# Tied scaling passes in a layer norm, later transposes, and twelve plain chunks instead of fourteen in an attention and GLU kernel

## The chip, the cores and the metric

The kernel runs on one core of a Trainium2 chip. The metric is device time of one execution in microseconds (us); the time before is the median of three runs. One execution was also taken with the hardware profiler, and all rows below are of that execution. Five engines work side by side: TensorE (PE, matrix products and transposes), VectorE (DVE), ScalarE (ACT), GpSimd (POOL) and SyncE (SP, which here only issues DMAs). Each engine runs its own instructions strictly in the order of its list, and waits at the head of the list when an operand is not there yet.

## The reference

Everything is fp32, with S = 2048 tokens of D = 576, 32 heads of 18, a window of 8 positions at distance 2, and F = 4608.

```python
def _A_ref(x, wqkv, wo):
    q, k, v = split_heads(x @ wqkv)
    idx = pos[:, None] - (jnp.arange(8) * 2)[None, :]
    logits = jnp.einsum("bhsd,bhswd->bhsw", q, k[idx]) * Dh ** -0.5   # masked where idx < 0
    o = jnp.einsum("bhsw,bhswd->bhsd", softmax(logits), v[idx])
    return o.reshape(B, S, D) @ wo
def _B_ref(x, w_gate, w_up, w_down):
    return (sigmoid(x @ w_gate) * (x @ w_up)) @ w_down
h = x + _A_ref(_layernorm(x), A_wqkv, A_wo)
return h + _B_ref(_layernorm(h), B_w_gate, B_w_up, B_w_down)
```

(`split_heads` and `k[idx]` stand for the reshapes and gathers of the reference.)

## The kernel before

Tokens are cut into four blocks of 512 (0 to 3). Every fp32 operand is split into a high and a low part (`split`: a copy on ACT, L104, and a subtraction on DVE, L105), and a product is made of three matrix products (high·high, low·high, high·low). A "token" product is the projection of 128 tokens (14 matmuls with 432 or 288 columns, lines 157 to 160); the four transposes that bring 128 normalised tokens into contraction order are line 146 and the small fifth one is line 150.

The program has these stages.

1. The front: the norm of a block (`ln1`) gives tiles `th` and `tl`; `qkv` projects it for one group of eight heads (four token products, copied out by ACT on line 397, stored to DRAM). For blocks 0 and 1 the norm's statistics are on DVE (`ln_j`). For blocks 2 and 3 they are on ACT and POOL: `ln_stats` makes a sum and a sum of squares (lines 133 and 134), POOL a power (135 to 137), and `ln_scale` two ACT passes (141 the scaling, 142 a copy of 64 columns). `norm_under` puts the norm of the next block between the token products of a `qkv`: block 2 under `qkv(1, 0)`, block 3 under `qkv(1, 1)`. Attention (`attention`, lines 189 to 226, nearly all DVE) of blocks 0 and 1 is stepped in between by `step(ag, n)`; `front` finishes block 0 (projection, norm).
2. The MLP. F is cut into 36 chunks of 128. A **std** chunk treats one block (`single`: 28 matmuls of 128x512 on lines 634 and 641), a **pair** chunk treats two blocks with seven products instead of eight (`pair`: 50 such matmuls). The down product of a chunk and a block is 24 matmuls of 128x288 on line 748, in the queue of `units`, on average one chunk later. The order is the list `items`: std of block 0 for the chunks below `NSTD`, pairs of blocks 0 and 1 for the chunks from there on, std of block 1 for the chunks below `NSTD`, and last all 36 pairs of blocks 2 and 3, whose down product has a form with seven products as well.
3. Under this a background (`bg`) is stepped. In the first std chunks, `under_first` ends the attention of block 1, projects it (`proj_scr`: loads `oj` from the attention's store in DRAM, transposes it, four token products for each half, residual, norm, transposes) and makes the pair's operands (`operands`: `s1` to `s4`). During the pairs, `under_rest` does the attention of blocks 2 and 3 (yielding `ATT`), and in the second std chunks it projects blocks 2 and 3 and makes the operands for the last pairs. `twice` calls `bg_step` eight times in a std chunk (six places, two of them twice).

The weights of a chunk are one load `wg` of 928 KB on SP (L590), issued as soon as its buffer is free, and split in `weights` (tiles `w`, `d`, 640, 256 and 384 columns a piece). The loads of the background (`oj`, `wow`, `hj`, L595) go through `paced`, which ties each behind the last load issued on the same queue. A tied instruction (`issue_after`) keeps its place behind another in the scheduler. The order of all else is set by the scheduler from the order of the code, priorities (`high_priority`), and when tiles come free.

Of the kernel before, what the change touches and what calls it, by code (L numbers as in the profile page):

```python
# [17 lines left out]
AF = mybir.ActivationFunctionType  # L18
# [3 lines left out]
P = 128  # L22
S = 2048
D = 576
# [6 lines left out]
NS = 4  # L31
# [19 lines left out]
END = object()  # L51
ATT = object()
HI = 400
HC = 700
NSTD = 14
NPL = 4
LAG = 3

# [2 lines left out]
def kernel(ctx, tc, x, wqkv, wo, wmlp, out):  # L61
# [41 lines left out]
    def split(hi, lo, src):  # L103
        act.activation(hi, src, AF.Copy)  # L104
        splits.append(dve.tensor_tensor(lo, src, f32(hi), ALU.subtract))  # L105

    def split_rest(t, src):
        act.activation(t, src, AF.Copy)
        dve.tensor_tensor(t[64:128], src[64:128], f32(t[64:128]), ALU.subtract)
# [20 lines left out]
    def ln_stats(xj, junk):  # L130
        mv = sm.tile([P, 2], F32, bufs=4, name="mv")
        rstd = sm.tile([P, 1], F32, bufs=4, name="rstd")
        act.activation(junk[:, :D], xj, AF.Copy, scale=-1.0 / D, accum_out=mv[:, 0:1])
        act.activation(junk[:, :D], xj, AF.Square, bias=mv[:, 0:1], accum_out=mv[:, 1:2])
        pool.tensor_scalar(rstd, mv[:, 1:2], 1.0 / D, EPS, ALU.mult, ALU.add)
        pool.tensor_tensor(rstd, rstd, mhalf, ALU.pow)
        pool.tensor_tensor(mv[:, 0:1], mv[:, 0:1], rstd, ALU.mult)
        return mv[:, 0:1], rstd

    def ln_scale(xj, nr, xn):  # L140
        act.activation(xn[:, :D], xj, AF.Identity, bias=nr[0], scale=nr[1])
        act.activation(xn[:, D:DX], xn[:, DM:D], AF.Copy)

    def tr_main(ps, xn):
        for c in range(4):
            pe.transpose(ps[:, c * P:(c + 1) * P], xn[:, c * P:(c + 1) * P], ident)
        return ps.rearrange("p (c n) -> p c n", c=4)

    def tr_rest(ps, xn):
        pe.transpose(ps[:, :P], xn[:, DM:DX], ident)  # L150
        return ps[:, :P]
# [193 lines left out]
    def ln1(b, xb):  # L345
        th = th3_tile(F32R) if b == 3 else th_tile()
        tl = tl_tile()
        yield th, tl
        xn = tok_tile()
        pri = 2 * HI if b == 0 else 0  # L350
        nr = []
        for j in range(NS):
            js = slice(j * P, (j + 1) * P)
            while b > 1 and len(nr) < min(j + 2, NS):
                nr.append(ln_stats(xb[:, len(nr)], xn[:, len(nr)]))
            with tc.high_priority(pri):
                if b > 1:
                    ln_scale(xb[:, j], nr[j], xn[:, j])
                else:
                    ln_j(xb[:, j], xn[:, j])  # L360
            pv = tr_main(mm_tile(), xn[:, j])
            pr = tr_rest(acc_tile(), xn[:, j])
            with tc.high_priority(pri):
                split(th[:, 0:4, js], tl[:, :, js], pv)
                split_rest(th[:, 4, js], pr)
            yield

    def raw_w(g):
# [21 lines left out]
    def qkv(b, g, T, w):  # L390
        e, hf = BLOCKS[b]
        ev = ev_tile([P, 3, NS, CG])
        for j in range(NS):
            ps = acc_tile()
            passes.append(tok_major(ps, NQ, *T, slice(j * P, (j + 1) * P), w[:, 0], w[:, 1]))
            with tc.high_priority(HI):
                act.activation(ev[:, :, j], ps[:, :NQ].rearrange("p (t c) -> p t c", t=3), AF.Copy)  # L397
# [36 lines left out]
    ag = att_all()  # L434
    T = []

    def norm_under(b, xb, call, n):
        gl = ln1(b, xb)
        T.append(next(gl))
        for _ in call:  # L440
            step(ag, n)
            next(gl, END)
            step(ag, n)
        drain(gl)

# [10 lines left out]
    w.append(qkv_w(1))  # L456
    xb = load_x(1)
    pads(0)
    norm_under(1, xb, qkv(0, 1, T[0], w[1]), 0)
    pads(1)  # L460
    xb = load_x(2)
    norm_under(2, xb, qkv(1, 0, T[1], w[0]), 1)
    xb = load_x(3)
    norm_under(3, xb, qkv(1, 1, T[1], w[1]), 1)
    wr = raw_w(2)
    heads(((2, 0), (3, 0)), w, 2)
    w.append(qkv_w(2, wr))
    wr = raw_w(3)
    pads(2)
# [373 lines left out]
    def proj_scr(pj, b, raw, wos, ins=None, after=None):  # L843
        e, hf = BLOCKS[b]
        th, tl = th_tile(), tl_tile()

        def tile_j(t, j):
            js = slice(j * P, (j + 1) * P)

            def put(pv, cs):  # L850
                if cs.start == 0:
                    if b < 2:
                        pool.dma_start(hacc[b][:, j], t[1])
                    else:
                        rows = slice(0, 7, 6) if b == 2 else slice(2, 5, 2)
                        pool.dma_start(hsev[:, j // 2, rows, j % 2],
                                       t[1].rearrange("p (i n) -> p i n", i=2))
                act.activation(raw[:, cs, js], pv, AF.Copy)

            yield from proj_j(bg_bank, t, wos, th[:, :, js], tl[:, :, js], lambda: t[0], put, (1, 0))  # L860

        todo = []
        if ins is None:
            ins = []
            for j in range(NS):
                ins.append([load_j(pj, b, j, 0), None])
                for _ in range(3 if b == 1 else 4):
                    yield
            ww = pj.tile([P, 2, 5, DH2], F32R, name="wow")
            paced(f32(ww), wscr[0])  # L870
            wos[0] = ww[:, 0], ww[:, 1]
            yield
            yield
            todo = list(range(NS))
        live = [tile_j(t, j) for j, t in enumerate(ins)]
        n = 0
        for _ in range(5):
            for gn in live:
                if todo and n % 2:
                    j = todo.pop(0)  # L880
                    ins[j][1] = load_j(pj, b, j, 1)
                n += 1
                next(gn)
                yield
        nxt = []
        for j, gn in enumerate(live):
            yield from gn
            if after is not None:
                nxt.append([load_j(pj, after, j, i) for i in range(2)])
        if b == 1:  # L890
            act.dma_start(xscr[b], raw[:, 0:2])
        return nxt
# [20 lines left out]
    def under_first():  # L913
        wos = [None, None]
        for _ in ag:
            if c >= 3 and wos[1] is None:
                wos[1] = wos_early()
            yield ATT
        at_stk.close()
        a1 = xt.tile([P, 5, TB], F32, tag="th", bufs=3, name="ar")  # L920
        with sb_pool("pj", "right") as pj:
            while c < 6:
                yield
            yield from proj_scr(pj, 1, a1, wos)
        with sb_pool("pp", "right") as pp:
            yield from operands(pp, 0, X, ("s2", "s3", "s1", "a11", "s4"), None, a1)
# [196 lines left out]

    def twice(i):
        bg_step(i)
        if i in (1, 4):
            bg_step(i)

    for c, (kind, p, f) in enumerate(items):
# [119 lines left out]
```

## Time and profile before

| | |
|---|---|
| device time, median of 3 | 1589.78 us (1589.67 to 1592.79) |
| profiled execution, device time | 1589.84 us |
| its span in the trace | 1588.0 us |
| granted TensorE clock, mean | 0.997 |
| PE busy | 1553.6 us (98%) |
| DVE busy | 1262.2 us (79%) |
| ACT busy | 872.7 us (55%) |

The span runs from the first to the last instruction of the trace; the device time is 1.84 us more. In the trace, "L157" is a line of the kernel, "acc<-qw,th" its output and inputs, and the bracket at the end of a row is the idle time before it and what released it. A chain shows in order of time which piece waited for which; the waits are grouped by waiting engine and releaser.

### The profile page before, as it was taken

The numbers are of one execution on the slowest core, as the hardware profiler recorded it, in microseconds if no ns is written. First come the engines' busy times: TensorE is split into PE (matmuls) and PEld (weight loads), VectorE is DVE, ScalarE is ACT, GpSimd is POOL, SyncE is SP. The second block draws the span as 40 slices with busy tenths as digits, with TensorE's granted clock in tenths as the row PEclk, the third lists the DMA queues.
The fourth block names the chain that finished last, engine by engine and source line by source line (L and its number), as shares of the span: only waits on it lengthen the run. The fifth ranks groups of instructions, "written<-read, shape, count | busy, mean of one in ns | idle before, by whom it ended". The sixth has DMA issues, their size and how long they took to land.

```text
span 1588.0 us, 22369 instructions
## 1 busy us (share of the span) xinstructions
PE 1553.6 (98%) x8532; PEld 1381.1 (87%) x8532; DVE 1262.2 (79%) x1891; ACT 872.7 (55%) x1568; POOL 193.7 (12%) x245
## 2 busy tenths in 40 slices
PE   7899999999999999999999999999999999999998
PEld 6899987888888888888889988888888888888887
DVE  6989999769999999999446678876677776677755
ACT  5632334425555565666443345776777676677761
POOL 1200000011000001000101100112111211112110
PEclk9999999999999999999999999999999999999999
DMA  7546554526467665665864234899889989989983
GB/s 273 204 155 216 215 184 165 205 81 256 109 161 198 163 160 155 167 176 148 217 195 153 90 112 121 181 181 180 172 175 188 176 171 182 176 168 184 183 173 120
DMA packets 76892, 273.50 MB, mean 172 GB/s; under 512 B 8336, under 2 KB 14224, under 8 KB 75888
## 3 DMA queue, kind: packets, MB, share of 16 engines
q0 software_dynamic: 27648, 104.94, 36.0%
q1 hardware_dynamic: 41504, 147.01, 27.2%
q10 hardware_dynamic: 7632, 20.12, 3.3%
q8 instruction: 67, 1.10, 0.3%
q14 instruction: 41, 0.34, 0.1%
HBM read 145.88 MB, written 128.52 MB: 173 GB/s over the span
## 4 chain that ended last, share of the span: by engine, by line
PE 86%; DVE 8%; DMA 3%; ACT 1%; issue 1%; POOL 1%; SPq 0%; ACTq 0%; DVEq 0%; POOLq 0%
PE b L634 41%; PE dp L748 14%; PE dp L810 11%; PE b L641 8%; PE acc L157 7%; PE b L157 1%; PE bgp L157 1%; DMA wg<-in_wmlp_dram 1%; DVE lg L193 1%; DVE pr L215 1%; DVE w L105 1%; PE acc L160 1%; PE acc L159 1%; DVE tl L105 1%; DVE pr L189 1%
## 5 line engine op out<-in xcount | busy, mean ns | idle before, releaser
L634 PE MATMUL b<-tl,w 128*128 128x512 f32 x1704 | 432.4, 393 | 0.0
L634 PEld LDWEIGHTS b<-tl,w 128*128 128x128 f32 x1704 | 308.8, 188 | 55.5 <-DVE s L654 0.3
L634 PE MATMUL b<-th,w 128*128 128x512 f32 x1356 | 349.4, 393 | 0.9 <-DVE s L723 0.8
L634 PEld LDWEIGHTS b<-th,w 128*128 128x128 f32 x1356 | 247.0, 188 | 46.7 <-DVE s L723 1.3
L104 ACT ACTIVATE w<-wg 128x384 fp32r<-128x384 f32 (+2 forms) x194 | 115.7, 598 | 119.8 <-PE b L641 59.4
L816 ACT ACTIVATE ev<-dp 128x576 f32<-128x576 f32 x224 | 144.9, 647 | 62.9 <-PE dp L810 58.6
L641 PE MATMUL b<-th,w 128*128 128x512 f32 x568 | 175.7, 390 | 0.0
L819 POOL DMA_DIRECT2D h<-ev x128 | 110.1, 860 | 458.5 <-ACT ev L816 442.6
L157 PE MATMUL acc<-qw,th 128*128 128x432 f32 x512 | 156.1, 366 | 1.6 <-DVE qw L105 1.2
L105 DVE TENSOR_TENSOR w<-wg,w 128x384 fp32r<-128x384 f32 (+2 forms) x194 | 125.2, 650 | 38.1 <-ACT w L104 38.0
L105 DVE TENSOR_TENSOR w<-tw,w 128x512 fp32r<-128x512 f32 x116 | 79.6, 687 | 81.3 <-ACT w L104 80.3
L641 PEld LDWEIGHTS b<-th,w 128*128 128x128 f32 x568 | 106.7, 188 | 23.4
L748 PE MATMUL dp<-d,h1h 128*128 128x288 f32 x640 | 120.0, 297 | 0.0
L748 PE MATMUL dp<-d,h0h 128*128 128x288 f32 x608 | 112.5, 295 | 0.8 <-DVE tail L758 0.8
L157 PEld LDWEIGHTS acc<-qw,th 128*128 128x128 f32 x512 | 98.1, 192 | 6.7 <-DVE qw L105 1.5
L748 PEld LDWEIGHTS dp<-d,h1h 128*128 128x128 f32 x640 | 99.6, 190 | 2.9
L756 ACT ACTIVATE stage<-dp 128x576 f32<-128x576 f32 x96 | 61.8, 647 | 66.0 <-PE dp L748 65.6
L748 PEld LDWEIGHTS dp<-d,h0h 128*128 128x128 f32 x608 | 93.6, 189 | 3.9 <-DVE tail L758 1.0
L104 ACT ACTIVATE w<-tw 128x512 fp32r<-128x512 f32 x116 | 72.8, 628 | 41.2 <-PE b L634 40.8
L157 PE MATMUL acc<-qw,tl 128*128 128x432 f32 x256 | 93.4, 365 | 0.0
L397 ACT ACTIVATE ev<-acc 128x432 f32<-128x432 f32 x64 | 33.9, 531 | 100.4 <-PE acc L160 93.9
L189 DVE TENSOR_TENSOR pr<-kw,q 128x2304 f32<-128x2304 f32 x32 | 81.7, 2552 | 3.2 <-DMA kw<-k 3.0
(292 smaller groups left out, 2938.6 us busy)
## 6 DMA issues: line engine op xcount, KB each, us to landing
h<-ev POOLq DMA_DIRECT2D x96, 576.0 KB, 7.3
wg<-in_wmlp_dram SPq DMA_DIRECT2D x49, 928.0 KB, 5.1
h<-stage POOLq DMA_DIRECT2D x24, 1152.0 KB, 10.2
wg<-in_wmlp_dram SPq DMA_DIRECT2D x36, 640.0 KB, 4.3
kw<-k SPq DMA_DIRECT2D x16, 792.0 KB, 4.7
vw<-v SPq DMA_DIRECT2D x16, 792.0 KB, 4.7
wd<-in_wmlp_dram SPq DMA_DIRECT2D x18, 576.0 KB, 7.4
h<-ev POOLq DMA_DIRECT2D x32, 288.0 KB, 6.7
```

The source lines that it names most:

```text
L104: act.activation(hi, src, AF.Copy)
L105: splits.append(dve.tensor_tensor(lo, src, f32(hi), ALU.subtract))
L157: pe.matmul(ps[:, :n], a[:, c, js], m[:, c], start=k == 0, stop=False)
L189: dve.tensor_tensor(pr, both(kw, u), q[:, us].unsqueeze(2).broadcast_to([P, 2, W, CG]), ALU.mult)
L397: act.activation(ev[:, :, j], ps[:, :NQ].rearrange("p (t c) -> p t c", t=3), AF.Copy)
L634: pe.matmul(ps, wt[:, a, k0 + c], xx[:, m + c], start=first and k == 0, stop=k == 5, skip_group_check=True)
L641: pe.matmul(ps, wt[:, a, k0], xx[:, 4], start=False, stop=a == 1, skip_group_check=True)
L748: pe.matmul(ps[:, i, :DH2], a[:, js], d[:, m, i * DH2:(i + 1) * DH2], start=k == 0, stop=k == n)
L756: act.activation(hv, ps, AF.Copy)
L810: pe.matmul(ps[:, i, :DH2], a[x][:, js], m[y], start=k in (0, 1, 3) and q == 0, stop=q == 2, skip_group_check=True)
L816: act.activation(hs[:, k % 2], ps[:, :, :DH2], AF.Copy)
L819: pool.dma_start(hsev[:, u, k0:k + 1], hs[:, :k + 1 - k0], accum_op=ALU.add, max_dma_last_dim=8 * D)
```

## The change

It has four parts.

- `NSTD` goes from 14 to 12. The list `items` has 84 entries instead of 86: chunks 12 and 13 of blocks 0 and 1, which were two std chunks of block 0 and, later, two of block 1, become two pair chunks.
- `twice` calls `bg_step` ten times in a std chunk instead of eight when the last step was not one of the attention. The first `proj_scr` starts from chunk 5 and not 6; its `oj` loads are 4 (block 1) or 7 (block 2) steps apart and not 3 or 4.
- In the norms of blocks 2 and 3 the scaling pass (L141) is tied behind the Square pass (L134) of the next tile.
- The transposes of those norms lag two tiles behind the scaling. The last two tiles of block 2 are transposed within `norm_under` of block 3 (ahead of its first transposes), the last two of block 3 under `qkv(2, 0)`.

```diff
-NSTD = 14
+NSTD = 12
...
     def ln1(b, xb):
...
+        lag = 2 if b > 1 else 0
         nr = []
-        for j in range(NS):
-            js = slice(j * P, (j + 1) * P)
-            while b > 1 and len(nr) < min(j + 2, NS):
-                nr.append(ln_stats(xb[:, len(nr)], xn[:, len(nr)]))
...
+        for k in range(NS + lag):
+            if k < NS and b > 1:
+                while len(nr) < min(k + 2, NS):
+                    nr.append(ln_stats(xb[:, len(nr)], xn[:, len(nr)]))
+                with tc.issue_after(getattr(nr[-1][2], "ins", nr[-1][2])):
+                    ln_scale(xb[:, k], nr[k], xn[:, k])
+            elif k < NS:
+                with tc.high_priority(pri):
+                    ln_j(xb[:, k], xn[:, k])
+            if k >= lag:
+                j = k - lag
...
-    def norm_under(b, xb, call, n):
+    def norm_under(b, xb, call, n, before=()):
         gl = ln1(b, xb)
         T.append(next(gl))
         for _ in call:
             step(ag, n)
+            drain(before)
             next(gl, END)
             step(ag, n)
-        drain(gl)
+        return gl
...
-    norm_under(2, xb, qkv(1, 0, T[1], w[0]), 1)
+    gl = norm_under(2, xb, qkv(1, 0, T[1], w[0]), 1)
     xb = load_x(3)
-    norm_under(3, xb, qkv(1, 1, T[1], w[1]), 1)
+    gl = norm_under(3, xb, qkv(1, 1, T[1], w[1]), 1, gl)
     wr = raw_w(2)
-    heads(((2, 0), (3, 0)), w, 2)
+    for _ in qkv(2, 0, T[2], w[0]):
+        next(gl, END)
+        step(ag, 2)
+    heads(((3, 0),), w, 2)
...
-                for _ in range(3 if b == 1 else 4):
+                for _ in range(4 if b == 1 else 7):
                     yield
...
-            while c < 6:
+            while c < 5:
                 yield
...
     def twice(i):
         bg_step(i)
-        if i in (1, 4):
+        if i in (1, 4) or phase is not ATT and i in (2, 5):
             bg_step(i)
```

The change moves instructions; three places are shown. The first is PE in the front, right behind the first token product of `qkv(1, 0)`, where `mm<-ident,tok` is a transpose of block 2 and `acc<-qw,th` a token product of block 1. Before:

```order
L157 MATMUL acc<-qw,th 128x432
L159 MATMUL acc<-qw,th 128x432
L160 MATMUL acc<-qw,th 128x432
L146 MATMUL mm<-ident,tok 128x128 x4
L150 MATMUL acc<-ident,tok 128x128
L157 MATMUL acc<-qw,th 128x432
```

With the change, at the same place:

```order
L157 MATMUL acc<-qw,th 128x432
L159 MATMUL acc<-qw,th 128x432
L160 MATMUL acc<-qw,th 128x432
L157 MATMUL acc<-qw,th 128x432
L157 MATMUL acc<-qw,tl 128x432
L157 MATMUL acc<-qw,th 128x432 x2
```

The transposes of block 2's first tile have left this place and stand two token products later; the others of blocks 2 and 3 lag likewise, and each pair of token products that they leave is run back to back.

The second is PE in the first std chunks, at the first transpose of the projection of block 1 (`b<-ident,oj`); `b<-tl,w` and `b<-th,w` are gate or up matmuls, and `dp` the down product. Before:

```order
L634 MATMUL b_2844<-tl,w_2744 128x512 x6
L634 MATMUL b_2844<-th,w_2743 128x512 x6
L641 MATMUL b_2844<-th,w_2743 128x512 x2
L146 MATMUL b_2898<-ident,oj 128x128 x4
L748 MATMUL dp<-d,h0h 128x288 x2
L748 MATMUL dp<-d,h0l 128x288 x2
```

With the change:

```order
L642 MATMUL b_2864<-tl,w_2752 128x512 x4
L146 MATMUL b_2832<-ident,oj 128x128 x4
L642 MATMUL b_2864<-tl,w_2752 128x512 x2
L146 MATMUL bgp<-ident,oj 128x128 x4
L642 MATMUL b_2864<-th,w_2751 128x512 x3
L146 MATMUL b_2871<-ident,oj 128x128 x4
L642 MATMUL b_2864<-th,w_2751 128x512 x2
L146 MATMUL bgp<-ident,oj 128x128 x4
L642 MATMUL b_2864<-th,w_2751 128x512
L649 MATMUL b_2864<-th,w_2751 128x512 x2
```

It is the same group of 14 gate and up matmuls (`b_2844`, now `b_2864`): the first transpose stood behind all 14, and now stands behind four, so ten of them come after it; the other three follow within the group, where they were spread over the next chunk.

The third is ACT in the second std chunks, at the copies of the transposes of block 2 (`th<-b`, `th<-bgp`) among the splits of the weights (`w<-wg`). Before:

```order
L678 ACTIVATE s<-b_7600 128x512
L104 ACTIVATE th<-b_7620 128x4x128
L104 ACTIVATE w_7709<-wg 128x640
L756 ACTIVATE stage<-dp 128x576
L104 ACTIVATE th<-bgp 128x4x128
L104 ACTIVATE w_7589<-wg 128x256
L104 ACTIVATE th<-b_7656 128x4x128
L104 ACTIVATE w_7588<-wg 128x384
L104 ACTIVATE th<-bgp 128x4x128
```

With the change:

```order
L104 ACTIVATE d<-wg 128x576
L104 ACTIVATE th<-b_7836 128x4x128
L686 ACTIVATE s<-b_7828 128x512
L104 ACTIVATE th<-bgp 128x4x128
L104 ACTIVATE th<-b_7862 128x4x128
L104 ACTIVATE w_7991<-wg 128x640
L104 ACTIVATE th<-bgp 128x4x128
L108 ACTIVATE th<-b_7906 128x128
L104 ACTIVATE w_7817<-wg 128x256
```

A 640-column split of newly loaded weights stood behind the first of the four copies, and a further one now stands behind the third; the first three copies have none between them. On SP the loads of the projection of block 2 there change from two `oj`, `wg`, two `oj`, `wg`, `wow`, three `hj`, `wg`, `hj` to two `oj`, `wg`, `oj`, `wg`, `oj`, `wow`, `wg`, four `hj`. In the first std chunks, where a `wg` stood behind the first of four `hj`, it now stands behind all four.

More of the change, by code (lines that the diff above doesn't have):

```diff
@@ L133, in ln_stats @@
         act.activation(junk[:, :D], xj, AF.Copy, scale=-1.0 / D, accum_out=mv[:, 0:1])
-        act.activation(junk[:, :D], xj, AF.Square, bias=mv[:, 0:1], accum_out=mv[:, 1:2])
+        sq = act.activation(junk[:, :D], xj, AF.Square, bias=mv[:, 0:1], accum_out=mv[:, 1:2])
         pool.tensor_scalar(rstd, mv[:, 1:2], 1.0 / D, EPS, ALU.mult, ALU.add)
@@ L137, in ln_stats @@
         pool.tensor_tensor(mv[:, 0:1], mv[:, 0:1], rstd, ALU.mult)
-        return mv[:, 0:1], rstd
+        return mv[:, 0:1], rstd, sq
     def ln_scale(xj, nr, xn):
@@ L350, in ln1 @@
         pri = 2 * HI if b == 0 else 0
+        lag = 2 if b > 1 else 0
         nr = []
-        for j in range(NS):
-            js = slice(j * P, (j + 1) * P)
-            while b > 1 and len(nr) < min(j + 2, NS):
-                nr.append(ln_stats(xb[:, len(nr)], xn[:, len(nr)]))
[L356 to L365, printed above, removed]
+        for k in range(NS + lag):
[9 more added lines that the diff above has]
+                j = k - lag
+                js = slice(j * P, (j + 1) * P)
+                pv = tr_main(mm_tile(), xn[:, j])
+                pr = tr_rest(acc_tile(), xn[:, j])
+                with tc.high_priority(pri):
+                    split(th[:, 0:4, js], tl[:, :, js], pv)
+                    split_rest(th[:, 4, js], pr)
             yield
@@ L458 @@
     pads(0)
-    norm_under(1, xb, qkv(0, 1, T[0], w[1]), 0)
+    drain(norm_under(1, xb, qkv(0, 1, T[0], w[1]), 0))
     pads(1)
     xb = load_x(2)
-    norm_under(2, xb, qkv(1, 0, T[1], w[0]), 1)
+    gl = norm_under(2, xb, qkv(1, 0, T[1], w[0]), 1)
     xb = load_x(3)
-    norm_under(3, xb, qkv(1, 1, T[1], w[1]), 1)
+    gl = norm_under(3, xb, qkv(1, 1, T[1], w[1]), 1, gl)
     wr = raw_w(2)
-    heads(((2, 0), (3, 0)), w, 2)
+    for _ in qkv(2, 0, T[2], w[0]):
+        next(gl, END)
+        step(ag, 2)
+    heads(((3, 0),), w, 2)
     w.append(qkv_w(2, wr))
```

## The prediction

> **What bounds the kernel now.** I read the busy times first, then PE's waits, then the stretches in which these waits fall, and last the chain around each.
>
> ```profile
> PE 1553.6 (98%) x8532; PEld 1381.1 (87%) x8532; DVE 1262.2 (79%) x1891; ACT 872.7 (55%) x1568; POOL 193.7 (12%) x245
> ```
>
> PE is the bound over the whole, so a change can only do two things: take matmuls away, or close the few holes in PE. The waits name the holes. (The columns are the waiting instruction, its releaser, total us, times, longest; the 9.1 us at the start, which nothing here touches, is left out.)
>
> ```profile
> PE bgp L146 <- DVE tl L105: 3.4, 1, 3.4
> PE mm L146 <- ACT tok L141: 2.6, 1, 2.6
> PE mm L157 <- DVE tl L105: 1.8, 1, 1.8
> PE acc L150 <- ACT tok L142: 1.8, 2, 1.0
> PE acc L157 <- DVE qw L105: 1.2, 1, 1.2
> PE bgp L150 <- DVE th L109: 1.1, 1, 1.1
> ```
>
> The rows of L141 and L142 are the norms of blocks 2 and 3: transposes that wait for the scaling on ACT, 2.6 + 1.8 = 4.4 us. The two `bgp` rows are the projections under the std chunks. Stretch by stretch (PE, PEld, DVE, ACT and POOL busy, granted clock, DMA share, GB/s):
>
> ```profile
> 40.00:300.00 260.00, 247.85 (x1309) 227.33 (x1309) 246.44 (x281) 100.57 (x217) 18.25 (x27) 0.99 0.52 183
> ...
> 40.00:60.00 20.00, 18.23 (x105) 16.88 (x105) 19.39 (x21) 14.07 (x38) 7.51 (x12) 1.00 0.65 223
> 60.00:80.00 20.00, 17.43 (x87) 16.15 (x87) 19.46 (x20) 10.05 (x25) 3.78 (x6) 0.91 0.54 183
> 300.00:320.00 20.00, 19.54 (x115) 16.75 (x113) 10.74 (x18) 8.72 (x18) 0.00 (x0) 1.00 0.77 295
> 320.00:340.00 20.00, 18.85 (x127) 17.91 (x128) 11.29 (x25) 3.69 (x7) 1.50 (x2) 1.00 0.17 63
> 800.00:820.00 20.00, 16.35 (x95) 13.92 (x94) 8.23 (x14) 9.22 (x18) 1.18 (x1) 0.99 0.90 281
> 820.00:840.00 20.00, 20.00 (x121) 18.68 (x122) 10.40 (x20) 6.33 (x14) 0.00 (x0) 0.92 0.24 88
> ```
>
> In the front (40 to 300) DVE is as full as PE, 246.4 against 247.9 of 260 us, and in the norms' two stretches fuller. Two stretches also run under a lowered clock. Cut to their edges, they and the stretches ahead of them are:
>
> ```profile
> 65.00:68.74 3.74, 1.17 (x8) 0.66 (x6) 3.65 (x4) 1.38 (x3) 2.63 (x3) 1.00 0.23 46
> 68.74:72.15 3.41, 3.41 (x12) 3.23 (x13) 3.25 (x6) 1.91 (x6) 0.00 (x0) 0.50 0.99 357
> 819.68:823.09 3.41, 3.15 (x13) 3.14 (x14) 2.70 (x6) 2.07 (x4) 0.00 (x0) 0.50 0.49 190
> ```
>
> So a hole in PE, 2.57 us idle out of 3.74, is followed by 3.41 us at half clock, which loses another 1.7 us. The 3.4 us hole at 819 has the same tail.
>
> **Part by part. Chunks.** The chain gives the price of a chunk (start, duration, count):
>
> ```profile
> 441.68 3.18 PE dp L748 x24
> 459.42 3.18 PE dp L748 x24
> ...
> 771.21 2.74 PE b L634 x12
> ...
> 790.35 2.74 PE b L634 x12
> ```
>
> The two `b` rows stand two std chunks apart, 19.14 us, so one is 9.57; the two `dp` rows stand one pair apart, 17.74. Two std chunks become one pair, twice: 2 x (17.74 - 19.14) = **-2.8 us**. PE was full in these stretches, so all of it counts.
>
> **Norms.** With the transposes two tiles behind the scaling, a token product of 2.7 us or two stand between; 4.4 us of waits and the 1.7 us of clock at 68.74 should go, 6.1 us on PE. But DVE decides when the attention of block 1 ends, and PE's gain reaches it at one place only:
>
> ```profile
> 88.55 0.66 DVE L205 TENSOR_REDUCE rs<-lg 128x32 f32<-128x256 f32 x1 [3.76 <-ACT lg L203]
> ...
> 87.68 0.53 ACT L397 ACTIVATE ev<-acc 128x432 f32<-128x432 f32 x1 [2.22 <-PE acc L160]
> 88.11 0.41 ACT L203 ACTIVATE lg<-lg 128x256 f32<-128x256 f32 x1
> ```
>
> DVE is idle 3.76 us because the exponential (L203) stands in ACT's list behind the copy of a token product (L397) that waits for PE. With PE 6.1 us ahead, the copy is early and the gap is what the exponential takes with its two hand-overs, some 0.45 us (0.41 and the start): DVE gains **-3.3 us**. The rest of PE's 6.1 comes back as wait: PE reaches the `qw` wait (1.2 us) earlier and waits about 1.2 + 6.1 - 3.3 = 4.0 us there.
>
> **The first std chunks.** From the attention's end a chain runs through two DMAs to the first transpose of the projection:
>
> ```profile
> 296.12 0.68 DVE kw L226
> ...
> 297.72 5.39 DMA o<-kw
> 303.25 2.80 DMA oj<-o
> 306.09 0.66 PE b L146 x4
> ```
>
> It moves 3.3 us up with DVE, to 302.8. In PE's new order this transpose has ten gate and up matmuls behind it that stood ahead of it, 10 x 2.74/12 = **+2.3 us** that PE still has to do when `oj` lands: it waits there for about that long, a wait that before has not. The 1.1 us wait of `bgp` L150 after it, and a shorter one behind that, came from
>
> ```profile
> 310.30 7.67 DMA wg<-in_wmlp_dram
> ...
> 321.13 0.31 DVE th L109
> ```
>
> weights landing late, with the copies of the transposes behind their split. All four `hj` are now ahead of the next `wg` and the split stands later in the lists, so I count **-1.5 us** (the idle PE time of the two stretches, 0.46 + 1.15, is the same). Against it, the products of the four tiles come one after the other with nothing between: each needs its copy, subtraction and residual first. The bounds are 0.5 (one hand-over of 0.3 to 0.5, as L109) and 3 us (a wait like that at 319 twice); I take **+1.5**, nearer to the wait that I saw.
>
> **The second std chunks.** Here is the largest hole:
>
> ```profile
> 805.93 10.52 DMA wg<-in_wmlp_dram
> ...
> 810.03 0.59 ACT L104 ACTIVATE th<-b 128x512 fp32r<-128x512 f32 x1
> 816.47 0.74 ACT L104 ACTIVATE w<-wg 128x640 fp32r<-128x640 f32 x1 [5.85 <-DMA wg<-in_wmlp_dram]
> ...
> 817.64 0.59 ACT L104 ACTIVATE th<-bgp 128x512 fp32r<-128x512 f32 x1
> ```
>
> ACT waits 5.85 us for weights that took 10.52 us, and the copy of a transpose is queued behind it; PE idles 3.65 us in 800 to 820 and loses 0.08 x 20 = 1.6 to the clock, 5.3 in all. In the new order the copies of two tiles have no such split ahead of them, the transposes come about 20 gate and up matmuls later, and the `oj` loads are spread. One split still stands ahead of the copy of the fourth. **-5.3 us**, and for what is left of it 0 to 5 (the whole again); I take **+1.5**: by the order its load is issued at about the first of the four transposes and the split's turn comes about 6 us later, an estimate from the matmuls between, while such loads land as this row of the page (count, size, median us) and the 10.52 above say:
>
> ```profile
> wg<-in_wmlp_dram SPq DMA_DIRECT2D x49, 928.0 KB, 5.1
> ```
>
> Mostly in time, then, and sometimes 4 us late.
>
> **Pair starts and other loads.** Two chunks fewer lie ahead of each start of pairs, so the operands (`s2`, first needed) have less time. Before, the third `bgp` transpose was at 357.18 and `s2` done at 370.9:
>
> ```profile
> 357.18 0.27 PE L150 MATMUL bgp<-ident,oj 128*128 128x128 f32 x1
> 369.65 1.22 DVE L105 TENSOR_TENSOR tl<-rs,tl 128x1024 fp32r<-128x1024 f32 x1
> ```
>
> 13.7 us. In the new order 84 gate and up matmuls (19.2 us) and 48 of the down product (6.4) lie between, 25.6 us: hidden. Without that cover it would cost up to those 13.7. For the second pairs it is 64 and 48, 21 us, against the same chain: hidden. The two more adds of 1152 KB into DRAM and the two fewer `wg` I count with small waits elsewhere at **+0.5** (-0.5 to 3, a wait like those above either way).
>
> **Sum.** -2.8 - 3.3 + 2.3 - 1.5 + 1.5 - 5.3 + 1.5 + 0.5 = -7.1 us. The span of 1588.0 becomes 1580.9, and the profiled time 1589.84 (1.84 beside its span, and 0.06 over the median of the runs) becomes **1582.8**. Its own bounds are 1.0 + 1.5 + 1.0 below and 1.5 + 3.5 + 2.5 above: 1579.3 to 1590.3.
>
> **A rule beside the rows.** The clock fell to 0.50 behind a longest gap of 2.58 us. The Trainium skill, "TensorE: Matmul & The Clock Gate", Part 1, says that the gate looks at a free-running window of about 3.4 us, and in its section on oscillation that gaps above about 3.4 us are to be avoided. The window's length agrees with the 3.41 us of the rows; the limit on a gap does not, since 2.58 was enough. By the limit the 4.0 us wait at `qw` would halve the clock and the 2.3 us wait at `oj` would not; by the rows either may.
>
> **Rivals.**
> (1) *The front gives nothing.* The gap of 3.76 us stays because another ACT entry or a load takes the exponential's place. For it: DVE also waits for loads in the front. Against: the gap's only releaser is that one row. +3.3: 1586.1.
> (2) *The whole of PE's gain arrives.* DVE has slack that its busy time hides, so that -6.1 takes the place of -3.3 + 2.3, and the dense products cost nothing, so that the +1.5 falls: 6.6 less, 1576.2. Against: DVE's 19.4 and 19.5 of 20 us in the norms.
> (3) *The clock follows the moved holes.* The wait at `oj` is over 2 us; one half-clock window behind it costs 1.7: 1584.5. (One at `qw` is eaten by the 1.8 us wait of `mm L157` behind it.)
> (4) *Slower: weights late again and again.* Twelve chunks carry the steps of fourteen, so loads and copies stand closer. Among the loads of 795 to 820 is
>
> ```profile
> wow<-wo SPq DMA_DIRECT2D x1, 1440.0 KB, 14.2
> ```
>
> and with the change a `wg` is right behind the `wow` on SP. If ACT's splits wait for `wg` ahead of transposes, each such place costs what 815 did, 5.3. One in the second std chunks instead of my 1.5, one more behind `wow`, and one in the first std chunks: 3 x 5.3 - 1.5 = +14.4, 1597.2. Two such places still give 1591.9, no change; from the third on it decides. Against: half of all `wg` land within 5.1 us.
>
> That the edit does nothing is out: the matmuls of four std chunks are gone from PE's order, those of two pairs are new, and the transposes have moved.
>
> **How the numbers follow.** 0.2% (3.2 us, about what a measurement can tell) is 1586.6 to 1593.0. Chances: forecast 0.50, (1) 0.17, (2) 0.13, (3) 0.10, (4) 0.10. Faster: nearly all of the forecast and of (3), all of (2), half of (1): 0.76. Slower: (4), 0.10. The rest, 0.14, is the same. The range goes to 1576 to hold (2), and above to 1591.5, the forecast's bound with (1) and a part of (4).
>
> **What would show it.** Right: no PE wait for `tok` L141 or L142 and no half clock near 68; a DVE gap under 1 us at L205 near 85; a PE wait of about 2 us for `oj`; no `bgp` wait over 1.5 us near 800; chunks at 9.57 and 17.74. Wrong: a PE wait over 3 us at a pair's start or in the std chunks with ACT standing at `w<-wg`, or DVE ending block 1's attention no earlier than 296.

## The result: 1586.72 us, 0.19% faster, less than half of what was forecast

| | before | changed |
|---|---|---|
| device time, median of 22 runs each | 1590.18 us | 1586.72 us |
| lowest to highest | 1585.66 to 1593.85 | 1583.3 to 1591.97 |
| ratio | | 0.9981, 95% interval 0.9973 to 0.9989 |
| profiled execution | 1589.84 us | 1591.97 us |

The gain is 3.0 us by the ratio (1.7 to 4.3) where 7.1 were forecast. The direction was right; the size was not. The changed kernel's first profiled execution is the longest of its 22, so a second one was taken (`again` below, 1586.86 us). Where the two traces differ, both numbers are given.

PE's waits in the changed kernel, largest first, without the start (in the first of the two executions):

```profile
PE acc L157 <- DVE qw L105: 2.8, 1, 2.8
PE b L146 <- DMA oj<-o: 2.8, 1, 2.8
PE mm L157 <- DVE tl L105: 2.7, 1, 2.7
...
PE b L146 <- DVE tl L105: 1.8, 1, 1.8
...
PE b L642 <- ACT s L712: 1.6, 1, 1.6
...
PE b L642 <- ACT s L722: 1.1, 2, 0.7
```

The waits for `tok` from L141 and L142 are gone, and so is the 3.4 us wait of `bgp`. In their place stand a longer wait for `qw`, the new one for `oj`, 1.8 us left in the second std chunks, and two that the prediction did not have: L712 and L722, which are copies of PSUM banks inside the **pairs**. The stretches that answer to those of before:

```profile
40.00:60.00 20.00, 20.00 (x114) 19.11 (x113) 19.48 (x19) 14.06 (x37) 3.05 (x9) 1.00 0.64 223
60.00:80.00 20.00, 19.43 (x107) 17.93 (x106) 19.43 (x21) 10.62 (x27) 5.11 (x6) 1.00 0.53 186
300.00:320.00 20.00, 17.25 (x93) 14.65 (x92) 11.02 (x20) 6.62 (x14) 0.00 (x0) 0.83 0.68 250
440.00:460.00 20.00, 18.40 (x101) 15.95 (x101) 16.69 (x17) 8.36 (x15) 1.58 (x2) 1.00 0.63 192
460.00:480.00 20.00, 19.32 (x104) 16.48 (x103) 19.86 (x29) 14.01 (x23) 1.20 (x1) 1.00 0.57 109
840.00:860.00 20.00, 18.03 (x118) 16.23 (x117) 12.73 (x23) 7.88 (x17) 0.00 (x0) 1.00 0.46 169
```

The norms' stretches, 40 to 80, are nearly full (20.00 and 19.43 of 20) and at full clock. PE is short of work in 300 to 320, with a clock of 0.83, and in 440 to 480, where before it was at 20.00 of 20. The 18.03 in 840 to 860 is what is left of the hole in the second std chunks.

To see where the sum failed, the trace is cut at the first gate matmul of a chunk (us; the last column ends with PE's last matmul). Two std chunks are 19.1 us less and two pairs 35.5 more, so "before, counted for 12" is what the second row would show if nothing but matmuls had changed.

| kernel | up to first std | first std | pairs of 0, 1 | second std | last pairs |
|---|---|---|---|---|---|
| before (14) | 231.6 | 155.0 | 384.5 | 185.6 | 626.8 |
| before, counted for 12 | 231.6 | 135.9 | 420.0 | 166.5 | 626.8 |
| changed | 231.1 | 138.0 | 423.9 | 163.3 | 629.4 |
| changed, `again` | 227.4 | 137.4 | 424.5 | 163.5 | 627.8 |

The second std chunks gained 3.0 to 3.2 us, the first lost 1.5 to 2.1, and the **pairs lost 3.9 to 4.5**. That is the larger part of the miss. It lies in three pairs: the sixth, the seventh and the last but one take 19.65, 18.95 and 18.75 us in the first execution and 21.57 (with half clock in it), 17.78 and 18.53 in `again`, where an undisturbed pair takes 17.75.

One boundary has moved with the work. The second std chunks hold 54 matmuls of the down product less (336 for 390), of which two chunks fewer account for 48; the other six stand in the last pairs (1584 for 1578). At 3.18 us for 24 that is 0.8 us, so like for like the second std chunks gained 2.2 to 2.4 us, and 0.8 of the last pairs' loss is work that came to them.

### The profile page after: what moved, and what is told of

It is laid out like the page before. It is cut to its first block, busy times and chain, and to the rows that moved or that the text cites. A ratio compares the mean times of both kernels' runs of the same rounds, so it can differ in the third digit from the quotient of the medians.

```text
span 1590.2 us, 22348 instructions
## 1 busy us (share of the span) xinstructions
PE 1554.2 (98%) x8520; PEld 1381.3 (87%) x8520; DVE 1258.0 (79%) x1889; ACT 877.4 (55%) x1576; POOL 193.7 (12%) x247
## 4 chain that ended last, share of the span: by engine, by line
PE 65%; DMA 4%; issue 3%; DVE 3%; ACT 1%; POOL 0%; SPq 0%; POOLq 0%; DVEq 0%; ACTq 0%
PE b L642 34%; PE dp L818 11%; PE dp L756 11%; PE b L649 6%; DMA wg<-in_wmlp_dram 2%; PE b L157 1%; PE bgp L157 1%; DVE w L105 1%; DMA h<-ev 1%; DMA tail<-h 0%; DMA o<-kw 0%; DVE s L662 0%; ACT w L104 0%; PE b L146 0%; DVE lg L193 0%
## 5 line engine op out<-in xcount | busy, mean ns | idle before, releaser
L104 ACT ACTIVATE w<-wg 128x384 fp32r<-128x384 f32 (+1 forms) x186 | 111.2, 601 | 106.2 <-PE b L649 52.4
L105 DVE TENSOR_TENSOR w<-wg,w 128x384 fp32r<-128x384 f32 (+1 forms) x186 | 121.1, 655 | 40.0 <-ACT w L104 39.7
L764 ACT ACTIVATE stage<-dp 128x576 f32<-128x576 f32 x104 | 67.2, 647 | 71.8 <-PE dp L756 71.1
```

The costliest lines, as they stand in the source:

```text
L764: act.activation(hv, ps, AF.Copy)
```

## Experiments

All ratios are to the kernel before, run beside each on the same chip.

**Again.** No edit.

> The changed kernel itself once more. Theory: the profiled execution at 1591.97 us was a long one of its kind (median 1586.72 of 22); the PE waits for L712 at 455 us (1.6) and 477 us (0.8) in the pairs and the 2.1 us more in the last 40 us were of that execution alone, and the holes at 129 us (qw), 190 us (tl) and 301 us (oj) with half clock behind them stand in every one. Then this profile has the three latter and not the former, and about 1586 to 1588 us. Rival: the waits of 455 and 477 us come from the order of the new chunks; then they are here again, at 1 us or more.

1586.62 us, 0.9978 (0.9966 to 0.999). The rival was right: near 450 us stands a PE wait of 1.9 us for L712 again, here with a window at half clock behind it. The 0.8 at 477 was not there. The holes in the pairs belong to the changed kernel, not to one execution.

**Norms alone.** `NSTD = 14`, `twice`, spacing and start as before; only the edits of `ln1` and `norm_under`.

> The tied scaling passes and late transposes alone, with 14 std chunks, eight steps in each and the old spacing of loads. Theory: PE gains some 6 us by 75 us, of which DVE takes 3.3 at the exponential near 85 us and keeps about 2 by the end of the attention of block 1; the second std chunks keep their 3.4 us hole. Time 0 to 2 us less than before (1588 to 1590). Rival (front worth nothing): the longer hole at the qw wait halves the clock, so the waits only move and the attention ends where it did: same as before within 1 us.

1585.66 us, 0.9976 (0.9964 to 0.9987): 3.8 us, more than I expected, and as much as the whole change. The std chunks start at 228.5 us, 3.1 earlier; pairs 384.5 as before.

**Chunks alone.** The rest of the change, norms as before.

> Twelve std chunks, ten steps, new spacing of loads and start at chunk 5, with the norms of before. Theory: -2.8 us from the matmuls, about -3 from the hole near 815 us, and some +4 from the first std chunks (a wait for oj of 2.5 us and half clock behind it): 1587 to 1589. Rival: the loss in the first std chunks comes with the front's shift only, since the attention's end and the transposes' place then meet otherwise: then no wait for oj over 1 us here and 1584 to 1586.

1589.11 us, 0.9998 (0.9986 to 1.001): nothing was gained that could be measured. Neither theory's count was right. The wait for `oj` is here too (2.5 us), so it does not come with the front's shift. First std chunks 136.6, pairs 423.6, second std 162.9 us: against the count for 12 the pairs lose 3.6 us and the first std chunks 0.7, while the second win 3.6 and the fewer matmuls save 2.7. By its stages this one execution is thus better than the median of its runs; its span is 1583.8 us and its time 1587.58, 3.8 us beside the span where the others have 1.8.

**Start at chunk 6.**

```diff
-            while c < 5:
+            while c < 6:
```

> The changed kernel with one edit undone: the projection of block 1 starts at chunk 6 again (the spacing of 4 stays). Theory: the first transpose no longer stands ahead of ten gate and up matmuls while oj is on its way, so the wait for oj and the two windows of half clock behind it (together some 6 us in the profile, of which 2.3 would be work done anyway) go: 2 to 4 us less than the changed kernel, 1583 to 1585. Rival: the projection is then late for the pairs' start, PE waits there for s2 or s4 by some us: 1587 or more.

1585.58 us, 0.9976 (0.9963 to 0.999), not told apart from the changed kernel. The wait for `oj` is gone, but 2.2 us come back a few us later, at the fifth transposes (first std chunks 136.2):

```profile
PE bgp L150 <- DVE th L109: 3.1, 2, 2.2
```

**The pairs' hole.** Here is SP's list in the changed kernel (only DMAs; start, issue time), then ACT:

```profile
409.59 5.66 SPq L598 DMA_DIRECT2D wg<-in_wmlp_dram  x2
430.06 0.33 SPq L178 DMA_DIRECT2D vw<-v  x1
446.23 0.33 SPq L177 DMA_DIRECT2D kw<-k  x1
446.66 0.37 SPq L598 DMA_DIRECT2D wg<-in_wmlp_dram  x1
```

```profile
452.71 0.74 ACT L104 ACTIVATE w<-wg 128x640 fp32r<-128x640 f32 x1 [3.50 <-DMA wg<-in_wmlp_dram]
...
455.98 0.60 ACT L712 ACTIVATE s<-b 128x512 f32<-128x512 f32 x1
```

The weights are issued at 446.66, at once after `kw`, an attention load that SP held for 15.8 us until the store of an earlier output had landed:

```profile
SPq L177 <- DMA o<-kw: 15.8, 1, 15.8
```

ACT then stands 3.5 us at the split, the bank copy L712 is queued behind it, and PE waits for the bank. The buffer that this `wg` fills had been free for 3.0 us, since DVE's last reading of it ended at 443.66:

```profile
442.91 0.75 DVE L105 TENSOR_TENSOR d<-wg,d 128x576 fp32r<-128x576 f32 x1
```

In the kernel before, the entries stand in the same order there:

```profile
422.35 10.57 SPq L590 DMA_DIRECT2D wg<-in_wmlp_dram  x2
441.94 0.33 SPq L178 DMA_DIRECT2D vw<-v  x1
449.16 0.33 SPq L177 DMA_DIRECT2D kw<-k  x1
455.20 0.33 SPq L590 DMA_DIRECT2D wg<-in_wmlp_dram  x1
```

```profile
454.37 0.75 DVE L105 TENSOR_TENSOR d<-wg,d 128x576 fp32r<-128x576 f32 x1
```

But `kw` was out 6 us before the buffer of the `wg` behind it came free, at 455.12, so that `wg` was not held. What changed is the place of the attention against the pairs. The first gate matmul of the pairs is at 386.6 us before and at 369.1 with the change, so `kw` goes out 62.6 us into the pairs before and 77.1 now; and between the first four attention loads of the pairs and this `vw` and `kw` stand three `wg` on SP's list where there were four. The hole near 450 us is in all six traces with twelve chunks and the attention's loads left as they were (1.4 to 1.9 us), and in none of the five kernels with fourteen. That two chunks fewer ahead of the pairs let the attention fall behind them is likely, but no run tests it apart.

Two edits test whether the held `wg` makes the hole. `pin` ties the loads of block 2, group 2, behind the last `wg`; `pin6` is `pin` with the start at chunk 6; `poolkv` issues the attention loads of blocks 2 and 3 from POOL.

```diff
-            if (b, g) == (1, 3):
+            if (b, g) in ((1, 3), (2, 2)):
```

> The changed kernel, with the loads of the attention of block 2, group 2, tied behind the last weight load issued ahead of them, so that on SP's list two weight loads and not one stand between vw_1 and kw_2. Theory: the hole of 1.6 to 2.1 us near 450 us and the 0.8 behind it, seen in all four kernels with twelve chunks and in none with fourteen, come from one weight load that stands behind kw_2, which itself waits for the store of the attention's output to land. Then both are gone, the stretch of 24 pairs falls from 424 to about 421 us, and the kernel is 2 to 4 us faster than the changed one (1583 to 1585). Rival: DVE is behind with the operands at the start of the pairs, and the loads only follow it; then the hole stays or moves and the time is as the changed kernel's, 1586 to 1588.

1584.33 us, 0.9969 (0.9957 to 0.9981); pairs 420.7 us, 0.7 above the count. Of the waits in the pairs one is left:

```profile
PE b L642 <- ACT s L722: 0.4, 1, 0.4
```

> The tie of the run before, and the projection of block 1 from chunk 6 again. Theory: both effects add, as they lie 130 us apart: no wait for oj over 1 us, no hole near 450 us; 1582 to 1584. Rival: the wait for oj is worth nothing, since PE waits for the same work a little later; then it equals the run before within 1 us.

1584.01 us, 0.9962 (0.9949 to 0.9975). First std chunks 134.8, pairs 422.9: no wait in them is over 0.4 us and all of them come to 1.2, so that most of the 2.9 us above the count is not explained. The times of the two are not told apart.

```diff
+            ld = pool if b > 1 else sp
-            sp.dma_start(q.rearrange("p j c -> p (j c)"), qscr[b][g])
+            ld.dma_start(q.rearrange("p j c -> p (j c)"), qscr[b][g])
```

(the same for `kw` and `vw`)

> The changed kernel, with the attention loads of blocks 2 and 3 (q, kw, vw) issued by POOL and not by SP, so that no weight load can stand behind them. Theory: the holes near 450 and 475 us are gone as with the tie, by another way: 24 pairs in about 421 us and 2 to 3 us off the changed kernel's time, 1583 to 1585. Rival: the holes come from DVE's load at the start of the pairs and stay; or the adds into DRAM, which POOL issues too, now stand behind the waiting loads, the buffers of the down product come free late and PE waits there instead: 1587 or more.

1583.45 us, 0.9955 (0.9942 to 0.9968); pairs 421.2 us, the hole near 450 us gone (0.8 us of L723 is left in two waits, the same copy in this kernel's numbering). Two quite different edits that only share that no `wg` stands behind `kw` at that place take some 3 us out of the pairs: the `wg` behind a held `kw` on SP's list is the cause of the hole. By its interval poolkv is faster than the changed kernel in its 22 runs, and touches the interval of `again`; for pin the times alone leave it open, and the trace decides.

**Twelve chunks with the old background.**

```diff
-        if i in (1, 4) or phase is not ATT and i in (2, 5):
+        if i in (1, 4):
```

(spacing and start as before too)

> The changed kernel's norms and twelve chunks, but with eight background steps a chunk, loads spaced 3 and 4 steps and a start at chunk 6, as with fourteen. Theory: the background then isn't done when the pairs start, what is left is drained there, and PE waits for operands by 3 to 10 us at the first pairs and again at the second: 1589 to 1597. Rival: the operands have 20 us to spare at both starts and the denser steps were not needed; then the holes at 450 and 839 us may go too and the time is 1582 to 1585.

1587.83 us, 0.9985 (0.9976 to 0.9994). The first std chunks take 133.8 us, less than with ten steps, and the second 165.8; the old 3.2 us wait of `bgp` is back and the pairs take 425.4. The time is that of neither expectation. No wait of 3 us at the pairs' start: the cover of some 20 us that I counted was there. The ten steps with wider spacing and the earlier start earn some 2 us in the second std chunks, the half clock behind the larger hole included, and by these traces cost 3.6 to 4.2 in the first.

**The wait for qw.** The fifth split stands behind a 2.5 us reduction on DVE.

```diff
-            with tc.high_priority(3 * HI if g == 0 else HI):
+            with tc.high_priority(3 * HI if g in (0, 2) else HI):
```

> The changed kernel with the splits of the third group's projection weights at the high priority that the first group's have, which also puts the fifth split of the fourth group ahead of a 2.5 us reduction on DVE. Theory: PE's wait of 2.9 us for qw near 129 us falls under 1 us and with it the half clock behind it (1.7 us); the stores of k come earlier, so DVE's 2.7 us wait for kw near 154 us shrinks, and the attention of block 1 ends 1 to 2.5 us earlier: 1 to 3 us off the time (1584 to 1586). Rival: DVE is the bound up to 300 us, the same 2.5 us reduction is only done later, and PE waits instead at the residual near 190 us; time as the changed kernel's.

1588.37 us, 0.999 (0.9981 to 0.9999): not faster than the changed kernel. The wait for `qw` falls to 0.3 us and others grow:

```profile
PE b L642 <- ACT s L686: 3.9, 1, 3.9
PE mm L157 <- DVE tl L105: 3.8, 1, 3.8
```

The rival was right: in the front PE's gain turns into wait at the next thing that DVE makes. (L686 is a sigmoid on ACT; it stands behind an exponential that waited 7.29 us for DVE.)

**The norms' two edits apart.**

```diff
-        lag = 2 if b > 1 else 0
+        lag = 0
```

> Of the norms' two edits the tie alone: scaling passes behind the next Square, transposes where they were before. Theory: PE still waits for the scaling at each transpose, since the tile is only just ready; 2 to 4 us of wait for tok in 45 to 70 us remain, and the time is that of before within 1 us (1589 to 1591). Rival: the late scaling passes of before (L141 behind two waits for POOL) are the whole cause and the tie removes the waits: under 1 us of them left and 1585 to 1587.

1588.21 us, 0.9985 (0.9975 to 0.9995), 2.4 us under the kernel before, where at most 1 was expected. The wait stays, moved to the small pass:

```profile
PE acc L150 <- ACT tok L142: 4.6, 3, 2.8
```

> Of the norms' two edits the lag alone. Theory: two token products between scaling and transpose are 5.5 us of cover against waits of at most 2.6 us, so the waits for tok go whatever the order on ACT; time as with both, 1585 to 1587. Rival: without the tie the scaling pass stands later on ACT by the same amount and waits of 1 us or more remain.

(`ln_scale` untied, lag of two.) 1586.48 us, 0.9966 (0.9954 to 0.9978), and no wait for `tok` from L141 or L142. By the waits the lag does the work; what the tie adds to it was not seen. By the times alone tie and lag are not told apart, as their intervals overlap.

**The rest of the second hole.** `wow` is moved behind the second `oj` load, on `pin6` (`pin6w`) and on norms alone (`normsw`):

```diff
                 ins.append([load_j(pj, b, j, 0), None])
+                if b == 2 and j == 1:
+                    ww = load_wow()
```

> The kernel with the tie at group 2 and the start at chunk 6, and the load wow (1440 KB) of the second projections moved ahead, behind the second oj load and not behind the fourth. Theory: the 2.0 us hole near 835 us has the cause that the 3.4 us hole of the kernel before had, a weight load that shares the DMA engines with wow (it landed after 9.4 us where others take 5), with the copies of the transposes behind its split on ACT. Then the load lands in about 5 us, the hole falls under 0.5 us, and the time is 2 us less than without the move: 1581 to 1583. Rival: the hole comes from the oj loads or the add of 1152 KB into DRAM; then the load stays at 8 to 10 us and the time is the same.

> Fourteen chunks with the new norms, and wow moved ahead in the same way. Theory: the 4.5 us hole near 811 us and the half clock behind it shrink to under 1 us, for 4 to 6 us off the kernel with the new norms alone (1580 to 1582), and twelve chunks are not what such a gain needs. Rival: as before, the load is late for other reasons; time 1585 to 1587.

1582.01 us, 0.9945 (0.9929 to 0.996), and 1587.54 us, 0.9973 (0.9962 to 0.9983). The hole stayed in both (1.8 and 4.5 us), and in `pin6w` the weight load still landed after 9.3 us: `wow` is not the cause, and the lower median of the first is not explained by it. What else runs there is an add of 1152 KB, issued at the moment of the weight load before it. (The kernel before has this add too: issued at 801.73, beside the load of 10.52 us that the prediction shows.) `noadd` leaves it out, so its result lacks that part:

> The kernel with the tie and the start at chunk 6, with one add of 1152 KB into DRAM left out: that of the last pair for block 1, which is issued near 819 us just ahead of the two weight loads of which the second lands after 9.4 us. Theory: the add shares the DMA engines with the weights; without it the second load lands in 5 to 6 us, ACT does not stand at its split, and the 2.0 us hole near 835 us is under 0.5 us. Rival: the oj load and the stores beside it are enough, or the hole is set by the place of the copies in ACT's list; then the load may land earlier but 1.5 us or more of the hole stay.

One run, 1580.83 us. The landing of that weight load in `pin6`, in `noadd`:

```profile
DMA to landing us min/median/max: 9.3/9.3/9.3
```

```profile
DMA to landing us min/median/max: 4.6/4.6/4.6
```

and ACT at its split, in the same order:

```profile
829.87 0.74 ACT L104 ACTIVATE w<-wg 128x640 fp32r<-128x640 f32 x1 [5.17 <-DMA wg<-in_wmlp_dram]
```

```profile
824.55 0.74 ACT L104 ACTIVATE w<-wg 128x640 fp32r<-128x640 f32 x1 [0.43 <-DMA wg<-in_wmlp_dram]
```

The hole is gone and the second std chunks take 161.4 instead of 162.9 us.

**All at once.** First POOL's loads, the start at chunk 6, and the add placed later in the code (`best`); then, on `pin6`, the add behind a copy that has to wait for a later result (`hold`):

> What the runs point to, together: the changed kernel with the attention loads of blocks 2 and 3 on POOL, the projection of block 1 from chunk 6 again, and the add of the last pair for block 1 held until the sixth of the second std chunks, when no weight load is urgent. Theory: the three holes lie apart (pairs 421 us as in poolkv, no wait of 2.7 us for oj, second std chunks 161 to 162 us as with the add left out), so the times add: 1580 to 1582, 9 to 11 us under the kernel before. Rival: the held add meets the weight loads or the second transposes instead and brings a hole of 2 us there; then 1582 to 1584.

1586.74 us, 0.9982 (0.9968 to 0.9996), a miss. The add had no reason to wait and POOL issued it where it was; and new waits came in the pairs (428.3 us), L723 3.6 us in three, whose cause was not followed up. Two edits that were good apart were not good together, since each moves the order of everything behind it.

```diff
+            if held and c == NF + 4:
+                mark = sm.tile([P, 1], F32, name="mark")
+                gate = pool.tensor_copy(mark, f32(hid[p][1][:, 0:1]))
+                with tc.issue_after(getattr(gate, "ins", gate)):
+                    add_dram(1, held.pop())
```

> The kernel with the tie at group 2 and the start at chunk 6, with the whole computation kept, and the last add for block 1 really held: POOL first copies one column of a result of the fifth of the second std chunks, and the add stands behind that copy in POOL's list. (In the run before, the add was only moved in the code; POOL still issued it at the same place, as its trace shows at 825.75 us with the weight load behind it landing after 9.44 us.) Theory: the second weight load lands in 5 to 6 us, the 2.0 us hole in the second std chunks is under 0.5 us and they take 161 to 162 us where the kernel without the hold takes 162.9; time 1 to 2 us under that kernel's 1584.0, 1581 to 1583. Rival: the held add of 13 us lies beside the next weight loads and makes another of them late; then the hole is one or two chunks later and the time is the same.

**1580.15 us, 0.9927 (0.9913 to 0.994)**: 11.6 us under the kernel before, and by its interval faster than the changed one. The add moves from 815.76 in `pin6` to

```profile
843.41 1.19 POOL L772 DMA_DIRECT2D h<-stage  x1 [0.28 <-issue]
```

the weights land after 4.6 us, and the stages are 227.3, 134.2, 422.3, 161.4 and 628.8. It is more than the stages explain: 1 to 2 us were expected of the hold and 1.5 are seen in the second std chunks, but 3.9 stand between the medians, 1584.01 and 1580.15, which were taken on two chips (5.6 by the two ratios). Its mean granted clock was 0.998 to 1.000 in its five runs, 0.996 to 0.998 in those of `pin6`, which goes the same way; the rest is open.

## Why the prediction was right or wrong, step by step

- **The sum.** 1589.84 - 7.1 is 1582.74, not 1582.8, which changes nothing here.
- **Chunks, -2.8.** Right: in the changed kernel the undisturbed chunks are at 9.56 and 17.75 us.
- **Norms, -3.3 through one gap on DVE.** Right in place, and in size within what the runs can tell. The gap is what I said it would be:

```profile
85.22 0.69 DVE L205 TENSOR_REDUCE rs<-lg 128x32 f32<-128x256 f32 x1 [0.48 <-ACT lg L203]
...
154.49 2.56 DVE L189 TENSOR_TENSOR pr<-kw,q 128x2304 f32<-128x2304 f32 x1 [2.68 <-DMA kw<-k]
```

  Two things I did not have: the gap at 107 us went as well, so that DVE was 4.4 us ahead by 113 us, and at 154.49 it gave 2.7 back, waiting for `kw`. What was left at the attention's end (its last L226, at 296.04 before) varies: 2.1 us in the first execution, 4.2 in `again`, where that wait for `kw` is missing, and 4.7 with the norms alone. The norms alone measured 3.8 us, and 3.3 lies within the interval (2.1 to 5.7). The wait at `qw` that I put at 4.0 us was 2.8 and 2.9.
- **First std chunks, +2.3.** Measured +1.5 to +2.1. The wait for `oj` was there at 2.6 to 2.8 us and the late-weights wait went, as said. The clock came on top in one execution and not in another: 3.4 us are lost behind 303 us in the first profile, none there in `again`. This is rival (3), which is a matter of the execution. The term can't be had apart from the front's: taken together the two stages were forecast at -1.0 and came to +1.6 in the first execution and -2.7 in `again`.
- **Second std chunks, -5.3 + 1.5 = -3.8.** Measured -3.0 to -3.2, and -2.2 to -2.4 without the work that moved on, with a hole of 1.8 left for the 1.5. The cause of the load's lateness that the prediction gave (spread of the `oj` loads) was not it; in the kernels with twelve chunks it was the add beside it, as `noadd` and `hold` showed.
- **Pair starts and other loads, +0.5.** This is **the step that failed**: 3.9 to 4.5 us in the pairs. I took for it "small waits elsewhere". I weighed the pairs' start for its operands, which were in time (`plain12` and all others), and looked at the order of SP at the std chunks only. I never read SP's list inside the pairs, although the pairs' attention loads wait there for stores, and one `wg` fewer between the first of them and the `kw` that held the list was there to be seen. In its place the runs show a `wg` held 3.0 us behind that `kw`, ACT standing 3.5 us at its split, and PE waiting 1.6 to 1.9 us for the copy behind the split; with the order changed the pairs take 420.7 (`pin`) and 421.2 us (`poolkv`). The right bound for the term lay in the rows: an ACT split standing 5.85 us at a `wg`.
- **Last pairs, 0.** 1.0 to 2.6 us more, of which 0.8 is the work that moved here. In the first execution another 1.7 is one window at half clock at 1563 us, behind a wait for `tail` of 1.9 us (0.8 before); in `again` the wait is 1.8 and no such window follows it there. Why that wait is longer stays open.
- **The rivals.** (1) is out for the norms. (2) is out: of PE's 6.1 us the norms alone brought 3.8 (2.1 to 5.7). (4) had the mechanism that decided, weights late with copies behind them, but put it at the std chunks, while it came in the pairs. Even so it did not make the kernel slower.
- **The clock gate.** The Trainium skill's limit of about 3.4 us for a gap ("TensorE: Matmul & The Clock Gate", oscillation) does not hold here as a limit below which the clock is safe: a gap of 2.95 us (the row of `again` below) was followed by half clock. That the window runs freely (Part 1 of the page) agrees with what follows. My 2.58 us was not the least either: the kernel before has a third window that I had not counted, 3.41 us at a mean clock of 0.51 from 253.12, behind a gap of 1.62 us, and at the same wait, there of 1.64 us, the changed kernel's first execution kept its clock.

## What to carry to other kernels

When one list carries loads of two kinds, one of which waits for a slow release, read that list through every stage after a change that shifts the work, not just at the places that were edited: one load in another place cost here some 3 us, as much as the fewer matmuls saved. By `noadd` and `hold`, large accumulating DMAs should be held away from loads that are needed within a few us, and held by something that really waits; later code is no later issue. And a hole closed on an engine that is not the bound is worth what the bound engine was waiting for it, which one row (the bound engine's idle time, with its releaser) gives.

## What was not expected of the hardware

The same hole halves the clock in one trace and not in another. In `again` and `poolkv`, which share the front's code but for the issuer of later loads, PE idles 2.95 and 2.77 us near 130 us, at the same wait for `qw`:

```profile
129.00:137.00 8.00, 5.05 (x18) 4.38 (x18) 7.96 (x5) 0.27 (x1) 0.00 (x0) 0.79 0.35 121
```

```profile
129.00:136.00 7.00, 4.23 (x22) 3.73 (x21) 6.97 (x5) 0.53 (x1) 0.00 (x0) 1.00 0.36 126
```

Clock 0.79 in the first, 1.00 in the second. Over the 22 runs of the changed kernel the mean granted clock goes from 0.995 to 0.999, and the mean time from 1589.8 us (four runs at 0.995) to 1585.0 (four at 0.999). One window costs 1.7 us, about 0.001 of the mean clock, so the spread from run to run goes with how many holes meet the window.

And an accumulating DMA of 1152 KB doubled the landing time of a 928 KB load issued 4.7 us after it, 9.3 for 4.6 us, though a `wow` of 1440 KB issued right behind that load cost it nothing that was seen.
